# Weight steps tied to their chunk's tanh, score products in turn, and wider attention stages in a fused attention and MLP kernel

## The chip, the core and the metric

The kernel runs on one core of one Trainium2 chip. The metric is the device time of one execution in microseconds, lower is better; the median of several runs counts. The engines are TensorE (PE), VectorE (DVE), ScalarE (ACT), GpSimd (POOL) and SyncE (SP), which issues the transfers.

## What is computed

```python
B, H, S, D = 4, 8, 576, 64
scores = q @ k.T / sqrt(D)             # per head; key within the last 64 positions
attn = exp(scores - max); attn /= sum + 1e-9
x = (attn @ v)                         # as 2304 tokens x 512
xn = x / sqrt(mean(x * x) + 1e-6) * rms_g
h = (silu(xn @ w_gate) * (xn @ w_val)) @ w_out     # d_ff 1536
t = h @ w_in2                                      # d_ff 2048
out = (t * sigmoid(1.702 * t)) @ w_out2
```

All of it is float32. The matrix products of the two MLPs are made as three products of split operands (high and low part).

## The kernel before

The 2304 tokens are six blocks of 384. Each block of the first MLP goes through 12 chunks of 128 hidden columns in two passes of six: in the first pass over the blocks chunks 0 to 5, with the attention of the next block woven in; in the second pass chunks 6 to 11. The second MLP then runs six blocks of 16 chunks. A chunk (L534 on) is a gate product `psg` of 12 matrix products (`proj`, L388), a tanh on ACT (L540), a combine on DVE (L541) that frees the bank of `psg`, a value product `psv` in the same form, a combine (L545), the split of the result in two parts (L548 on ACT, L549 on DVE), and 12 output products (`emit_O`, L509) one chunk later. `psg` and `psv` have one bank each.

Attention works in 18 stages `m` of 128 tokens. The steps of a stage are the transposes of its keys and queries (`att_Tk`, `att_Tq`: L234 and L243 on PE, copies L228 on ACT), 32 score products of 64x64 (`att_S`, L263) into two banks, one per parity of head (`e`), then eight reduces on DVE (L281), eight exps on ACT (L293) and the scaling (L303 to L305), transposes of the result (`att_PT`, L313), value products (`att_PV`, L328), the copy to `xraw` (L336 or L338), the squares (`rms_sq`, L345 to L349), and, once a block, the RMS scaling (`rms_scale`: products with `ones` L359, L362, POOL L363, L365, L369) and the split of the block into `xh` and `xl` (`split_x`, L377 to L381). `at_slot` puts each step into one of 18 slots of a block's first pass, three per chunk; the first three stages stand at the start, before any chunk. Their tiles come from a pool of two PSUM banks. `NLD` = 4 load buffers hold keys, queries and values in the order of `ld_order`.

The weights are float32 in HBM and are split on the chip by 34 weight steps (`w_step`: ACT L142 and L143, DVE L144, L145 and L148; then `w_half`: ACT L126 and DVE L127). 9 of them belong to the first half of the first MLP, 18 to the first MLP as a whole. Slots call them: in block 0 every even slot, up to step 9, later two per block. Three staging buffers hold what SP has loaded.

The order of each engine's instructions is set by a scheduler that simulates the program. `tc.issue_after(ins)` puts what is written in it behind `ins` on the queue of `ins`' engine. Before, the first of the steps 2 to 9 alone, on ACT, is put behind `hold[0]`, which is the last ACT cast of the first block's split; the others stand where the scheduler puts them. `pe_hold` is the last product of the start's RMS scaling.

Of the kernel before, what the change touches and what calls it, by code (L numbers as in the profile page):

```python
# [12 lines left out]
AF = mybir.ActivationFunctionType  # L13
# [4 lines left out]
N_FREE = 1  # L18
# [5 lines left out]
def window_attention__gated_mlp__mlp_kernel(  # L24
# [86 lines left out]
    def w_load(limit):  # L111
        while w_next[0] < min(limit, n_w):
# [6 lines left out]
            staged.append(st)  # L119

    def w_half():
        if not half:
            return
        pair, w24 = half.pop()
        w = wp.tile([128, 2, 1024], F32R, tag="w", name="w")
        nc.scalar.copy(w[:, 0, :], w24.bitcast(F32))  # L126
        nc.vector.tensor_tensor(w[:, 1, :], w24.bitcast(F32), w[:, 0, :].bitcast(F32), ALU.subtract)  # L127
        for e, key in enumerate(pair):
            weights[key] = w[:, :, e * 512:(e + 1) * 512]

    def w_step(limit):
# [8 lines left out]
        m = tmp.tile([128, 1024], I32, tag="tmp", name="m")  # L140
        with tc.issue_after(hold[0]) if N_FREE < w_next[1] <= n_wh else nullcontext():
            nc.scalar.mul(hi.bitcast(F32), hi.bitcast(F32), 2.0 ** -112)  # L142
# [16 lines left out]
    for m in range(lead):  # L159
        ld_order += [("v", 2 * m), ("v", 2 * m + 1)]  # L160
    for m in range(lead, NG // 2):
        ld_order += [("k", m), ("q", m), ("v", 2 * m), ("v", 2 * m + 1)]
    ld_next = [0]
# [93 lines left out]
    def att_S(m):  # L257
        QT = qts[m]
        banks = [att_bank("s") for _ in range(2)]
        for hp in range(NHP):  # L260
            for g in range(2):
                for e in range(2):
                    nc.tensor.matmul(  # L263
                        banks[e][64 * g:64 * g + 64, hp * 128:(hp + 1) * 128],
                        QT[64 * e:64 * e + 64, hp, 64 * g:64 * g + 64],
                        KT[64 * e:64 * e + 64, hp, key_blocks(2 * m + g), :],
                        start=True,
                        stop=True,
                    )
        first = next((g for g in range(2) if (2 * m + g) % GPB == 0), None)  # L270
# [152 lines left out]
    def at_slot(j, s, fn):  # L423
        slots.setdefault(j * NS + s, []).append(fn)
# [8 lines left out]

    def first_S(m):
        with tc.issue_after(pe_hold):
            att_S(m)

    for b in range(1, NB):
        for i in range(TB // 128):
            m = b * TB // 128 + i  # L440
            s0 = 4 * i if b == 1 else 6 * i - 4
            lag = 3
            at_slot(b - 1, s0, lambda m=m: (first_S if m == TB // 128 else att_S)(m))
            if m + 1 < NG // 2:
                at_slot(b - 1, s0 + 2, lambda m=m + 1: att_Tk(m))
                at_slot(b - 1, s0 + 3, lambda m=m + 1: att_Tq(m))
            at_slot(b - 1, s0 + lag, lambda m=m: att_PT(m))
            at_slot(b - 1, s0 + lag + 1, lambda m=m, b=b, i=i: att_PV(m, x_of(b)[0], i * 128))
            at_slot(b - 1, s0 + lag + 2, lambda b=b, i=i: rms_sq(x_of(b)[0], i * 128, x_of(b)[1]))
        at_slot(b - 1, s0 + lag + 3, lambda b=b: rms_scale(*x_of(b), 0, TB))  # L450

    if True:
# [30 lines left out]
        for m in range(T0 // 128):  # L483
            att_S(m)
            att_Tk(m + 1)
            att_Tq(m + 1)
        for m in range(T0 // 128):
# [11 lines left out]
        for ps_i in range(2):  # L499
            f_lo, f_hi = ps_i * FH, (ps_i + 1) * FH  # L500
            for j in range(NB):
# [32 lines left out]
                for f in range(f_lo, f_hi):  # L534
# [4 lines left out]
                    a = ap_.tile([128, TB], F32, tag="a", name="a")  # L539
                    nc.scalar.activation(a, psg[:, :T], AF.Tanh, scale=0.5)  # L540
                    nc.vector.scalar_tensor_tensor(a, a, 1.0, psg[:, :T], ALU.add, ALU.mult)  # L541
# [129 lines left out]
```

## Time and profile before

| | us |
|---|---|
| median of 3 runs | 1056.81 |
| range of the runs | 1056.78 to 1059.46 |
| profiled execution | 1059.42 |
| its span | 1057.6 |
| PE busy in the span | 1010.6 |

The profile is one execution. Busy times of an engine are sums of its instructions; a window of the trace gives them for a stretch. "PEclk" is the granted clock of TensorE as a share of full speed. An idle time in brackets behind a row is what the engine stood before the instruction, with what ended it.

### The profile page before, as it was taken

The numbers are of one execution on the slowest core, as the hardware profiler recorded it, in microseconds if no ns is written. First come the engines' busy times: TensorE is split into PE (matmuls) and PEld (weight loads), VectorE is DVE, ScalarE is ACT, GpSimd is POOL, SyncE is SP. The second block draws the span as 40 slices with busy tenths as digits, with TensorE's granted clock in tenths as the row PEclk, the third lists the DMA queues.
The fourth block names the chain that finished last, engine by engine and source line by source line (L and its number), as shares of the span: only waits on it lengthen the run. The fifth ranks groups of instructions, "written<-read, shape, count | busy, mean of one in ns | idle before, by whom it ended". The sixth has DMA issues, their size and how long they took to land. (4 is left out here: it accounts for less than half of the span.)

```text
span 1057.6 us, 15454 instructions
## 1 busy us (share of the span) xinstructions
PE 1010.6 (96%) x6158; PEld 938.8 (89%) x6158; DVE 515.6 (49%) x1132; ACT 411.0 (39%) x884; POOL 13.2 (1%) x39
## 2 busy tenths in 40 slices
PE   6888599999999989999999999999999999999997
PEld 5778499898989989999999998899999989988896
DVE  5598983645445489644334389232232332322222
ACT  6688874543444346511112145222222222322222
POOL 2000000000000000000000000000000000000000
PEclk9599699898999999999999999999999999999999
DMA  9476971423223065522022052001010010000000
GB/s 236 128 210 209 274 224 41 122 59 100 62 70 90 2 226 175 167 90 86 5 90 90 29 180 100 1 10 50 1 60 1 1 60 1 29 2 2 31 1 30
DMA packets 113320, 88.43 MB, mean 84 GB/s; under 512 B 77664, under 2 KB 104288, under 8 KB 113248
## 3 DMA queue, kind: packets, MB, share of 16 engines
q1 hardware_dynamic: 113248, 87.44, 27.9%
q8 instruction: 48, 0.79, 0.3%
q14 instruction: 24, 0.20, 0.1%
HBM read 68.55 MB, written 18.87 MB: 83 GB/s over the span
## 5 line engine op out<-in xcount | busy, mean ns | idle before, releaser
L614 DVE TENSOR_TENSOR a<-a,psh 128x384 f32<-128x384 f32 x96 | 53.1, 553 | 207.8 <-ACT a L613 207.8
L598 PE MATMUL acc<-w,gh 128*128 128x512 f32 x576 | 153.0, 397 | 0.0
L388 PE MATMUL psh<-x2h,w 128*128 128x384 f32 x768 | 152.6, 339 | 0.2 <-DVE a L614 0.2
L388 PEld LDWEIGHTS psh<-x2h,w 128*128 128x128 f32 x768 | 137.2, 188 | 3.2 <-DVE a L614 0.5
L613 ACT ACTIVATE a<-psh 128x384 f32<-128x384 f32 x96 | 47.1, 491 | 223.7 <-PE psh L388 223.0
L598 PEld LDWEIGHTS acc<-w,gh 128*128 128x128 f32 x576 | 107.1, 188 | 18.5
L509 PE MATMUL acc<-ah,w 128*128 128x384 f32 x576 | 118.9, 343 | 0.3 <-ACT ah L548 0.3
L509 PEld LDWEIGHTS acc<-ah,w 128*128 128x128 f32 x576 | 102.8, 190 | 1.3 <-ACT ah L548 0.8
L541 DVE SCALAR_TENSOR_TENSOR a<-a,psg 128x384 f32<-128x384 f32 x72 | 39.7, 551 | 106.6 <-ACT a L540 106.4
L388 PE MATMUL psh<-x2l,w 128*128 128x384 f32 x384 | 86.2, 338 | 0.0
L598 PE MATMUL acc<-w,gl 128*128 128x512 f32 x288 | 85.2, 396 | 0.0
L540 ACT ACTIVATE a<-psg 128x384 f32<-128x384 f32 x72 | 35.4, 491 | 118.5 <-PE psg L388 118.5
L618 DVE TENSOR_TENSOR gl<-a,gh 128x384 fp32r<-128x384 f32 x96 | 53.5, 558 | 55.6 <-ACT gh L617 45.0
L388 PE MATMUL psg<-xh,w 128*128 128x384 f32 x288 | 69.0, 374 | 11.0 <-ACT xh L379 5.6
L617 ACT CAST gh<-a 128x384 fp32r<-128x384 f32 x96 | 49.3, 513 | 67.9 <-DVE a L614 51.1
L388 PEld LDWEIGHTS psh<-x2l,w 128*128 128x128 f32 x384 | 69.9, 188 | 5.9
L388 PEld LDWEIGHTS psg<-xh,w 128*128 128x128 f32 x288 | 55.1, 206 | 16.1 <-ACT xh L379 7.7
L548 ACT CAST ah<-a 128x384 fp32r<-128x384 f32 x72 | 36.9, 512 | 75.4 <-DVE a L545 75.1
L509 PE MATMUL acc<-al,w 128*128 128x384 f32 x288 | 65.7, 342 | 0.0
L388 PE MATMUL psv<-xh,w 128*128 128x384 f32 x288 | 65.4, 355 | 0.2 <-DVE a L545 0.2
L598 PEld LDWEIGHTS acc<-w,gl 128*128 128x128 f32 x288 | 54.2, 189 | 12.6
L388 PE MATMUL psv<-x2h,w 128*128 128x384 f32 x288 | 58.5, 339 | 0.1
(104 smaller groups left out, 1460.3 us busy)
## 6 DMA issues: line engine op xcount, KB each, us to landing
st<-in_moe_w_out_dram SPq DMA_DIRECT2D x28, 512.0 KB, 5.1
o<-x2s SPq DMA_DIRECT2D x48, 192.0 KB, 1.9
st<-in_moe_w_in_dram SPq DMA_DIRECT2D x16, 512.0 KB, 5.0
st<-in_moe_w_gate_dram SPq DMA_DIRECT2D x12, 512.0 KB, 4.9
st<-in_moe_w_val_dram SPq DMA_DIRECT2D x12, 512.0 KB, 5.8
qkv<-in_v_dram SPq DMA_DIRECT2D x20, 256.0 KB, 3.0
x<-xraw SPq DMA_DIRECT2D x6, 768.0 KB, 4.7
xr<-x SPq DMA_DIRECT2D x6, 768.0 KB, 4.3
```

The source lines that it names most:

```text
L388: nc.tensor.matmul(ps[:, :T], w[:, wi, c * 128:(c + 1) * 128], xx[:, c, :T], start=(i == 0), stop=(i == 3 * KC - 1),)
L509: nc.tensor.matmul(acc[c][:, :T], w[:, wi, c * 128:(c + 1) * 128], aa, start=(f == f_lo and pi == 0), stop=(f == f_hi - 1 and pi == 2),)
L540: nc.scalar.activation(a, psg[:, :T], AF.Tanh, scale=0.5)
L541: nc.vector.scalar_tensor_tensor(a, a, 1.0, psg[:, :T], ALU.add, ALU.mult)
L548: nc.scalar.copy(ah, a)
L598: nc.tensor.matmul(acc[c], (gh, gh, gl)[pi][:, c * 128:(c + 1) * 128], w[:, (0, 1, 0)[pi], :], start=(f == 0 and pi == 0), stop=(f == NF2 ...
L613: nc.scalar.activation(a[:, :T], psh[:, :T], AF.Sigmoid, scale=1.702)
L614: nc.vector.tensor_tensor(a[:, :T], a[:, :T], psh[:, :T], ALU.mult)
L617: nc.scalar.copy(gh[:, :T], a[:, :T])
L618: nc.vector.tensor_tensor(gl[:, :T], a[:, :T], gh[:, :T].bitcast(F32), ALU.subtract)
```

## The change

The change has four parts. First, the ACT part of every weight step after the first is put behind `hold[0]`, and `hold[0]` is the tanh of the chunk in which the step is called, except in block 0, where it stays the last cast of the split. Second, the 32 score products of a stage are chained on PE, so that head pair by head pair and quarter by quarter (the two halves `g` of the queries, the two parities `e` of heads) each stands behind the one before. Third, the slots of an attention stage lie further apart, and a block's stages begin earlier. Fourth, keys and queries of the second block's first stage are transposed in slot 0 of block 0, behind `pe_hold`, instead of at the start; and loads of keys and queries now come before the values of the stage before.

```diff
-        with tc.issue_after(hold[0]) if N_FREE < w_next[1] <= n_wh else nullcontext():
+        with after(hold[0] if w_next[1] > N_FREE else None):
             nc.scalar.mul(hi.bitcast(F32), hi.bitcast(F32), 2.0 ** -112)
...
+    ld_order += [("k", lead), ("q", lead)]
     for m in range(lead, NG // 2):
-        ld_order += [("k", m), ("q", m), ("v", 2 * m), ("v", 2 * m + 1)]
+        if m + 1 < NG // 2:
+            ld_order += [("k", m + 1), ("q", m + 1)]
+        ld_order += [("v", 2 * m), ("v", 2 * m + 1)]
...
+        prev = None
         for hp in range(NHP):
-            for g in range(2):
-                for e in range(2):
-                    nc.tensor.matmul(
+            for g, e in ((0, 0), (0, 1), (1, 0), (1, 1)):
+                with after(prev):
+                    prev = nc.tensor.matmul(
...
-    def first_S(m):
+    def held(fn, m):
         with tc.issue_after(pe_hold):
-            att_S(m)
-
+            fn(m)
+
+    m = TB // 128
+    for fn in (att_Tk, att_Tq):
+        at_slot(0, 0, lambda m=m, fn=fn: held(fn, m))
     for b in range(1, NB):
         for i in range(TB // 128):
             m = b * TB // 128 + i
-            s0 = 4 * i if b == 1 else 6 * i - 4
-            lag = 3
...
+            if b == 1:
+                s0, lags = 1 + 4 * i, (2, 3, 4, 5, 5, 6)
+            else:
+                s0, lags = 6 * i - 7, (2, 3, 5, 7, 8, 9)
+                if b == 2 and i == 0:
+                    s0, lags = -5, (2, 3, 3, 5, 6)
...
+            at_slot(h, s0 + lags[2], lambda m=m: att_PT(m))
+            at_slot(h, s0 + lags[3], lambda m=m, b=b, i=i: att_PV(m, x_of(b)[0], i * 128))
+            at_slot(h, s0 + lags[4], lambda b=b, i=i: rms_sq(x_of(b)[0], i * 128, x_of(b)[1]))
+        at_slot(h, s0 + lags[5], lambda b=b: rms_scale(*x_of(b), 0, TB))
...
         for m in range(T0 // 128):
             att_S(m)
-            att_Tk(m + 1)
-            att_Tq(m + 1)
+            if m + 1 < T0 // 128:
+                att_Tk(m + 1)
+                att_Tq(m + 1)
...
-                    nc.scalar.activation(a, psg[:, :T], AF.Tanh, scale=0.5)
+                    tanh = nc.scalar.activation(a, psg[:, :T], AF.Tanh, scale=0.5).ins
+                    if ps_i or j:
+                        hold[0] = tanh
```

The order of instructions moves in three places that matter below. The first is ACT at the start, around the first weight's scaling; `quad`, `p` and `sm` are the scores, `pt`, `KT` and `QT` the transposed tiles, `st` a weight. Before:

```order
L293 ACTIVATE quad,sm<-quad,sm 128x128 x2
L228 COPY pt<-ps_t 128x512
L293 ACTIVATE quad,sm<-quad,sm 128x128 x2
L228 COPY pt<-ps_t 128x512
L142 ACTIVATE st<-st 128x1024
L143 ACTIVATE st<-st 128x1024
L293 ACTIVATE quad,sm<-quad,sm 128x128 x5
L228 COPY quad<-ps_t 128x512
L293 ACTIVATE quad,sm<-quad,sm 128x128 x3
```

The same place after (L234 for L228, L300 for L293, L145 and L146 for L142 and L143):

```order
L234 COPY pt<-ps_t 128x512
L300 ACTIVATE quad,sm<-quad,sm 128x128 x8
L234 COPY pt<-ps_t 128x512
L300 ACTIVATE quad,sm<-quad,sm 128x128 x4
L145 ACTIVATE st<-st 128x1024
L234 COPY quad<-ps_t 128x512
L300 ACTIVATE quad,sm<-quad,sm 128x128
L146 ACTIVATE st<-st 128x1024
L300 ACTIVATE quad,sm<-quad,sm 128x128 x2
```

The weight's scaling now stands behind five more of the start's exps. The second place is ACT around the tanh of block 0's last chunk. Before, weight steps stand behind it:

```order
L540 ACTIVATE a<-psg 128x384
L228 COPY QT<-ps_q 128x512
L126 CAST w<-m 128x1024 x2
L548 CAST ah<-a 128x384
L228 COPY pt<-ps_t 128x512
L142 ACTIVATE st<-st 128x1024
L143 ACTIVATE st<-st 128x1024
L228 COPY pt<-ps_t 128x512
L142 ACTIVATE st<-st 128x1024
L143 ACTIVATE st<-st 128x1024
L582 ACTIVATE x2s<-acc_548 128x384
L336 COPY xraw<-ps_v 128x4x128
```

After (L559 is the tanh, L569 the cast of L548, L603 the output's copy, L343 the copy of L336):

```order
L559 ACTIVATE a<-psg 128x384
L234 COPY pt<-ps_t 128x512
L569 CAST ah<-a 128x384
L234 COPY pt<-ps_t 128x512
L146 ACTIVATE st<-st 128x1024
L603 ACTIVATE x2s<-acc_532 128x384
L300 ACTIVATE p,sm<-p,sm 128x128 x8
L343 COPY xraw<-ps_v 128x4x128
L603 ACTIVATE x2s<-acc_534 128x384
L352 ACTIVATE s_1197<-xraw 128x512
L234 COPY KT<-ps_k 128x4x128
L234 COPY QT<-ps_q 128x512
```

No weight is cast any more in this place, and a stage's eight exps stand in a row. The third place is PE at a score stage; the number behind `ps_s` is its bank's tile. Before, at the boundary from block 2 to 3:

```order
L509 MATMUL acc2_1330<-al_1868,w_1216 128x384
L509 MATMUL acc3_1331<-al_1868,w_1216 128x384
L263 MATMUL ps_s_1798<-KT_93,QT_92 64x128 x8
L359 MATMUL ps_r_1783<-ones_88,sq_1349 128x1
L263 MATMUL ps_s_1799<-KT_93,QT_92 64x128 x8
L365 MATMUL ps_r_1783<-ident_87,ry_1788 128x128 x3
L234 MATMUL ps_k_1883<-ident_87,qkv_1745 128x128 x4
L388 MATMUL psg_1962<-xh_1871,w_558 128x384
```

After, at a stage of block 0:

```order
L320 MATMUL ps_t_741<-ident_87,p_635 128x128 x4
L320 MATMUL ps_t_748<-ident_87,p_635 128x128 x4
L270 MATMUL ps_s_755<-KT_93,QT_92 64x128
L395 MATMUL psg_794<-xh_520,w_717 128x384 x4
L270 MATMUL ps_s_756<-KT_93,QT_92 64x128
L270 MATMUL ps_s_755<-KT_93,QT_92 64x128
L270 MATMUL ps_s_756<-KT_93,QT_92 64x128
L270 MATMUL ps_s_755<-KT_93,QT_92 64x128
```

The products into one bank stood together, and now the two banks alternate from the second product on. (One row of this listing can stand for two instructions of the trace.)

## Rows read from the trace of the kernel before

**Rows 1.** Page, busy time and share of the span per engine.

```profile
PE 1010.6 (96%) x6158; PEld 938.8 (89%) x6158; DVE 515.6 (49%) x1132; ACT 411.0 (39%) x884; POOL 13.2 (1%) x39
```

**Rows 2.** Windows: length, busy PE, PEld, DVE, ACT, POOL, PEclk, DMA share, GB/s.

```profile
0.00:46.60 46.60, 34.08 (x330) 28.47 (x330) 20.98 (x92) 28.53 (x78) 7.89 (x34) 0.75 0.84 190
46.60:105.26 58.66, 52.13 (x376) 48.56 (x372) 54.78 (x118) 48.53 (x100) 0.00 (x0) 0.94 0.69 202
105.26:141.80 36.54, 23.93 (x184) 20.81 (x184) 36.35 (x65) 29.76 (x50) 1.90 (x1) 0.72 0.77 246
415.00:1057.60 642.60, 636.17 (x3315) 594.59 (x3313) 250.36 (x439) 178.32 (x328) 0.00 (x0) 1.00 0.14 49
```

**Rows 3.** Timeline of the start (start, duration, idle before): ACT, SP, PE.

```profile
21.21 1.10 ACT L142 ACTIVATE st<-st 128x1024 f32<-128x1024 f32 x1 [3.13 <-DMA st<-in_moe_w_val_dram]
...
34.18 0.58 ACT L228 COPY quad<-ps_t 128x512 f32<-128x512 f32 x1 [0.23 <-PE ps_t L313]
37.13 1.16 ACT L143 ACTIVATE st<-st 128x1024 int32<-128x1024 uint32 x1 [2.37 <-DMA st<-in_moe_w_val_dram]
...
40.46 0.63 ACT L345 ACTIVATE s<-xraw 128x512 f32<-128x512 f32 x1
...
29.31 1.28 SPq L201 DMA_DIRECT2D qkv<-in_k_dram  x2
...
22.30 0.66 PE L234 MATMUL ps_k<-ident,qkv 128*128 128x128 f32 x4 [2.66 <-DMA qkv<-in_k_dram]
...
46.61 0.69 PE L388 MATMUL psg<-xh,w 128*128 128x384 f32 x1
```

**Rows 4.** Windows of the exps alone (L293, ACT), then the reduces (L281, DVE).

```profile
46.60:105.26 58.66, 9.92 (x48) 0.94 0.69 202
...
46.60:105.26 58.66, 5.55 (x48) 0.94 0.69 202
```

**Rows 5.** Weight steps on DVE: windows of L144 and L145, timeline DVE, PE.

```profile
46.60:105.26 58.66, 6.71 (x10) 0.94 0.69 202
105.26:141.23 35.97, 4.03 (x6) 0.72 0.78 249
...
46.60:105.26 58.66, 12.09 (x10) 0.94 0.69 202
...
104.01 1.22 DVE L148 CUSTOM_DVE_ANT_0 m<-st,m 128x2048 uint16<-128x2048 uint16 x1
...
108.44 2.35 DVE L127 TENSOR_TENSOR w<-m,w 128x1024 fp32r<-128x1024 f32 x2
...
141.82 1.68 PE L388 MATMUL psg<-xh,w 128*128 128x384 f32 x8 [0.21 <-DVE a L541]
```

**Rows 6.** Timeline of the boundary from block 4 to 5, DVE and PE.

```profile
364.72 0.69 DVE L338 COPY xraw<-ps_v 128x512 f32<-128x512 f32 x1 [2.16 <-PE ps_v L328]
...
366.64 0.29 DVE L349 TENSOR_TENSOR sq<-s 128x128 f32<-128x128 f32 x1
...
369.05 0.28 PE L359 MATMUL ps_r<-ones,sq 128*128 128x1 f32 x2
...
373.11 0.45 PE L388 MATMUL psg<-xh,w 128*128 128x384 f32 x1 [1.60 <-ACT xh L379]
```

**Rows 7.** Boundary from block 2 to 3: two windows, and the timeline of PE.

```profile
248.20:262.66 14.46, 12.83 (x81) 11.33 (x80) 9.20 (x33) 6.79 (x25) 0.85 (x1) 0.76 0.48 147
251.00:257.00 6.00, 5.58 (x33) 4.77 (x34) 4.30 (x17) 4.51 (x18) 0.00 (x0) 0.56 0.35 103
...
251.03 1.34 PE L263 MATMUL ps_s<-KT,QT 64*64 64x128 f32 x16 [1.12 <-DVE sm L281]
...
255.19 0.69 PE L388 MATMUL psg<-xh,w 128*128 128x384 f32 x1 [0.40 <-ACT xh L379]
```

**Rows 8.** Timeline of PE: score products of a start stage and of a later one.

```profile
15.68 1.10 PE L263 MATMUL ps_s<-KT,quad 64*64 64x128 f32 x32
...
68.21 1.09 PE L263 MATMUL ps_s<-KT,QT 64*64 64x128 f32 x16
```

More of the change, by code (lines that the diff above doesn't have):

```diff
@@ L119, in w_load, with after @@
             staged.append(st)
+    def after(ins):
+        return tc.issue_after(ins) if ins is not None else nullcontext()
     def w_half():
@@ L268, in att_S @@
                         stop=True,
-                    )
+                    ).ins
         first = next((g for g in range(2) if (2 * m + g) % GPB == 0), None)
@@ L440, in window_attention__gated_mlp__mlp_kernel @@
             m = b * TB // 128 + i
-            s0 = 4 * i if b == 1 else 6 * i - 4
-            lag = 3
-            at_slot(b - 1, s0, lambda m=m: (first_S if m == TB // 128 else att_S)(m))
-            if m + 1 < NG // 2:
[L445 to L450, printed above, removed]
+            if b == 1:
[4 more added lines that the diff above has]
+                    s0, lags = -5, (2, 3, 3, 5, 6)
+            h = b - 1
+            if m == TB // 128:
+                at_slot(h, s0, lambda m=m: held(att_S, m))
+            else:
+                at_slot(h, s0, lambda m=m: att_S(m))
+            if m + 1 < NG // 2:
+                at_slot(h, s0 + lags[0], lambda m=m + 1: att_Tk(m))
+                at_slot(h, s0 + lags[1], lambda m=m + 1: att_Tq(m))
+            at_slot(h, s0 + lags[2], lambda m=m: att_PT(m))
+            at_slot(h, s0 + lags[3], lambda m=m, b=b, i=i: att_PV(m, x_of(b)[0], i * 128))
+            at_slot(h, s0 + lags[4], lambda b=b, i=i: rms_sq(x_of(b)[0], i * 128, x_of(b)[1]))
+        at_slot(h, s0 + lags[5], lambda b=b: rms_scale(*x_of(b), 0, TB))
     if True:
```

## The prediction

> **What bounds the kernel now.** I read the busy shares first: TensorE (PE) is busy 96% of the span [rows 1], so only the stretches in which it is not at work, or not at full clock, can give anything. The windows by stage [rows 2] say where those are. From 415 us to the end PE works 636.17 of 642.60 us at a granted clock of 1.00, and the order of all engines is the same there in both kernels: nothing to win or lose. Three stretches ahead are different. In the start (0 to 46.6 us) PE has 34.08 us at a clock of 0.75 and ScalarE (ACT) and the transfers set the pace. In block 0 up to the combine (L541) of its sixth chunk (46.6 to 105.26) VectorE (DVE) is busy 54.78 of 58.66 us. From there to block 1's second chunk (105.26 to 141.8) DVE is busy 36.35 of 36.54 us, and PE does 23.93 at 0.72. Those 141.8 us are where the waits are; between 142 and 415 PE is near its limit except at the block boundaries.
>
> The sum is made against the profiled execution, 1059.42 us (span 1057.6 and 1.82 around it). The median of the runs is 1056.81, 2.61 lower, and I take the same savings off it. Under 0.3%, about 3.2 us, a measurement of this kernel can't tell a change from none.
>
> **A, the start: -3.4.** ACT reaches the first weight's scaling (L142) at 21.21 after standing 3.13 us for its DMA, with exps of stage 2 queued behind it [rows 3]. The changed order has 21 of the 24 start exps ahead of the corresponding instruction, 16 before, and the two copies of the second block's first keys and queries are gone from the start. An exp costs 0.41 us (9.92 over 24, [rows 4]), so 5 x 0.41 = 2.1 and two copies of about 0.57 each = 1.1: the last transposed copy, at 34.18, comes 3.2 us earlier. The PE wait of 2.66 us at 22.30 for the block's keys goes with them. What is late next is the fourth ACT weight instruction (L143, at 37.13 after 2.37 us for its DMA): in the new order it stands between the copy of xraw and the Square of 40.46. SP issues that DMA some 1.3 us earlier, since the two half loads of k(4) (1.28 us at 29.31) no longer stand right ahead of it, so about 35.8 + 1.16 = 37.0, against 40.46: -3.4. The moved transposes (4 in 0.66, twice) come ahead of the first gate product in place of stage 3's score products. First gate product: 46.61 becomes about 43.2. If the DMA lands when it did, I get -2.2; if it doesn't bind, -6. The DMA queue (SP) is passed too: k(4) and q(4) now come before v(6) and v(7), and the latter wait for the release of k(3) and q(3); the value products that need them are some 20 us later, so I cost that at nothing; were that cover gone it would be one load, about 2.66.
>
> **B, block 0 to the sixth combine: -3.7.** Weight steps cost DVE, per step, 6.71/10 = 0.67 (L144), 12.09/10 = 1.21 (L145), 1.22 (L148) and 2.35/2 = 1.18 (L127) [rows 5]: 4.28 us. Now every step waits for the tanh of its chunk or, in block 0, for the last cast of the first block's split; by the sixth combine the order has 2 L144, 2 L145 and 1 L148 fewer (-1.3 - 2.4 - 1.2 = -5.0) and one scaling of a stage's exps (L304, L305) more, which I put at +1.3 since L305 passes over 1024 columns as L145 does. DVE's 54.78 becomes 51.1; with the same 3.9 idle the stretch takes 55.0 instead of 58.7. From 52 (no idle) to 58.7 (ACT or the weight's DMA takes over) is possible. Behind the tied L142 on ACT stand L143, exps and copies, and for it waits the weight chain of DVE, not PE until that weight's chunk comes; that is why I cost the tie itself at nothing.
>
> **C, from there to block 1's second chunk: -12.5.** Six whole weight steps (6 L144 in 4.03, [rows 5]) stand here before and none now: 6 x 4.28 = 25.7 of DVE's 36.35 us. DVE then has about 10.7 us of work and no longer bounds; the chain into the next block does. 16 output products at 0.21 (8 of a like shape in 1.68, [rows 5]) and the score products 1.1 beside transposes: +5. Then the eight exps of the stage, now in a row on ACT, 8 x 0.41 = 3.3: +8.3. The last copy of xraw, the Square and the two sums took from 364.72 to 366.93 at a boundary without neighbours [rows 6], 2.2, with half a us of latency: +11. From the first product with ones to the first gate product there took 369.05 to 373.11, 4.06 [rows 6]: +15.1. From a block's first gate product to its second chunk's took 255.19 to 262.66, 7.5 [rows 7], and the one stage of score products and reduces that falls into it (reduces 5.55/3 = 1.85 per stage, [rows 4]) costs perhaps 1.5: 24 us instead of 36.5. Bounds: 19 (PE's 23.93 at a clock of 0.72 is 17.2 at 1.00, plus 1.60 of idle) and 28.5 (each of the eight exps and reduces is paid in full on the way). Second chunk: 141.82 becomes 122.2.
>
> **D, the boundaries from block 1 to 4: -1.0.** Each loses about 4.7 us [rows 7]: 14.46 - 12.83 = 1.63 idle, and 12.83 x (1 - 0.76) = 3.1 by the clock, 0.56 in six of these us, a mean between the two levels of 2.4 and 1.2 GHz. The 1.12 us wait for the second bank of scores goes, as the boundary's score stage now has its banks in turn; but on ACT eight exps (3.3) instead of four (1.65) stand ahead of the next tanh, which takes away 1.65. So each lies between +0.5 and, if PE stays warm and only the 1.60 of [rows 6] is left, -3.1; for three of them between +1.5 and -9.3. I take a third of 1.12 each, -1.0, since the rms chain that sets the first gate product is untouched. The boundary 4 to 5 has no score stage: 0.
>
> **E, score products in turn: -11.1.** Stage 2 in the start ran 32 score products in 1.10 us; 15 later stages show two groups of 16, one bank each, of 1.09 [rows 8]. The changed order alternates the banks in all of them: the first product, then 15 when the second bank is free, then 16. So 2 x 1.09 - 1.10 = 1.08 less, minus the single product that stands alone, 1.09/16 = 0.07: 1.01. Stages 7 to 17 lie in the PE-bound stretch, 11 x 1.01 = 11.1; stages 3 to 6 are in A to C. The price of it is that the 15 products, and the output products queued behind them on PE, wait until DVE has freed the second bank; before, 16 products waited there as well (1.12 us at 251.03, [rows 7]), so I add nothing. Bounds 0 to 11.9.
>
> A rule speaks against E. The Trainium skill, TensorEngine Tiling (Array Packing), "PSUM Bottleneck", says that tiling speeds up TensorE but not the evacuation of PSUM, which can become the limit after it; by that rule E would be 0. Its "Tiling Modes" has four independent 64x64 tiles, with which the 1.10 against 2.18 us of [rows 8] agree.
>
> **Sum.** 3.4 + 3.7 + 12.5 + 1.0 + 11.1 = 31.7: 1056.81 - 31.7 = 1025.1 (for an execution like the profiled one 1027.7). The second MLP stays at 642.6 us.
>
> **Rivals.** *More at start and boundaries* (0.20): PE stays at full clock through three boundaries (9.3 instead of 1.0) and the weight's DMA doesn't bind in the start (6.0 instead of 3.4): 10.9 more, 1014.2. For it speaks that a stall is what precedes the drop of 0.56; against it that ones to first gate product still leaves PE 1.60 us idle where no score stage stands. *Block 0 stays as long* (0.15): DVE gets lighter but waits for ACT and for the weights' DMA instead, B is 0 and C only 8: 1033.3. For it: ACT is busy 48.53 of 58.66 in B [rows 2]; against it: DVE is the busier. *Packing is hidden* (0.05): DVE's reduces take 1.85 us a stage, more than the 1.01 saved, so if PE waits for them anyway, E is 0: 1036.2. Against it: DVE is busy 49% of the span [rows 1], most of it early, and PE has other products to go on with. *Slower* (0.05): the tanh of a chunk stands behind eight exps, and PE has a single bank for the gate product, so each stage could stall PE up to 3.3 us. It decides from 31.7/15 = 2.1 us per stage on; at the full 3.3, 15 x 3.3 = 49.5 is lost and 31.7 won: 1074.6. Against it: the bank is needed again only after a value product and an output product, 12 + 12 products at up to 0.21, some 5 us. That the order isn't what the diff says is excluded by the order shown above.
>
> **Chances and range.** The forecast has 0.55, the rivals 0.20, 0.15, 0.05 and 0.05. The forecast's own bounds, A 2.2 to 6, B 0 to 6.7, C 8 to 17.5, D -1.5 to 9.3, E 10 to 11.9, don't fall together; half of their width around the sum and the first three rivals give 1009 to 1040. Faster by over 0.3%: 0.94, from all but the slower rival and 0.01 of the others; within it 0.02 (several terms at their poor ends); slower 0.04.
>
> **What would show it.** First gate product near 43 (A); about 55 us to the sixth combine (B); no L147 (the shift of before's L144) between block 0's sixth combine and block 1's second chunk, which starts near 122 (C); each stage's score products after the first block in one stretch of 1.1 us, but for the first product (E); boundaries of 13 to 14 us (D); 642.6 us for the second MLP. The prediction is wrong if PE's waits before a gate product grow to some us in each stage (tanh behind exps), if the sixth combine stays near 105, or if PE stays busy just as long in the later blocks though the products are packed.

## The result, and the profile of the changed kernel

The changed kernel takes 1032.69 us (median of 4 runs, 1028.16 to 1033.24), the kernel before 1057.84 beside it; the ratio is 0.9752, interval 0.972 to 0.9783. The profiled executions are 1032.62 and 1059.42 us: 26.8 us less, with spans of 1030.8 and 1057.6. 1025.1 was predicted, with a range of 1009 to 1040, and 31.7 us less. All times of stretches below are of one profiled execution each.

In the changed kernel the lines have moved: L559 is the tanh, L562 the combine that frees the bank of `psg`, L270 the score products, L288 the reduces, L300 the exps, L310 to L312 their scaling, L345 the copy to `xraw`, L366, L370, L372 and L376 the RMS chain, L386 the cast to `xh`, L145 and L146 the weight step on ACT, L395 the projections, L528 the output products.

The page's first part after, against [rows 1]: PE works 22 us less, DVE 1 and ACT 3 us less.

```profile
PE 988.7 (96%) x6158; PEld 916.8 (89%) x6158; DVE 514.5 (50%) x1132; ACT 408.1 (40%) x884; POOL 12.4 (1%) x39
```

The windows after that answer to [rows 2], cut at the same events (first gate product, sixth combine, second gate product of block 1), and the second MLP; columns as there:

```profile
0.00:44.03 44.03, 32.45 (x298) 27.49 (x299) 20.46 (x91) 27.09 (x75) 7.91 (x34) 0.72 0.86 189
44.03:98.37 54.34, 50.24 (x395) 46.31 (x394) 51.73 (x115) 45.80 (x99) 0.00 (x0) 0.91 0.68 200
98.37:125.04 26.67, 21.57 (x218) 17.89 (x216) 15.16 (x58) 14.87 (x48) 0.86 (x1) 0.94 0.59 164
388.40:1030.80 642.40, 635.91 (x3312) 593.98 (x3310) 268.47 (x456) 194.85 (x344) 0.00 (x0) 1.00 0.16 56
```

The third row is the plainest: DVE was busy 36.35 of 36.54 us there, and now 15.16 of 26.67. The events themselves, from the timelines of ACT, PE and DVE:

```profile
37.37 1.13 ACT L146 ACTIVATE st<-st 128x1024 int32<-128x1024 uint32 x1 [1.59 <-DMA st<-in_moe_w_val_dram]
...
44.03 0.67 PE L395 MATMUL psg<-xh,w 128*128 128x384 f32 x1
...
98.37 0.55 DVE L562 SCALAR_TENSOR_TENSOR a<-a,psg 128x384 f32<-128x384 f32 x1
...
125.04 1.68 PE L395 MATMUL psg<-xh,w 128*128 128x384 f32 x8 [1.12 <-DVE a L562]
```

| stretch | before | after | change | predicted |
|---|---|---|---|---|
| A, to the first gate product | 46.61 | 44.03 | -2.6 | -3.4 |
| B, to the sixth combine | 58.65 | 54.34 | -4.3 | -3.7 |
| C, to block 1's second gate product | 36.56 | 26.67 | -9.9 | -12.5 |
| the rest of the span (D and E) | 915.8 | 905.8 | -10.0 | -12.1 |

By stretches the sum looks like a good forecast with each term a little off. The experiments show that this holds for one of its five terms. How far one execution can be trusted shows in two pairs of kernels of the experiments. The changed kernel and a_chain_inner have the same order of instructions up to 117 us, and A took 44.0 and 42.6 us in them, B 54.3 and 52.8. The kernels a_nochain and best2 have the same order up to 330 us, and C took 26.3 and 29.0. Differences of that size in one stretch say little.

### The profile page after: what moved, and what is told of

Read it like the earlier page. It is cut to its first block, busy times and chain, and to the rows that moved or that the text cites. A ratio compares the mean times of both kernels' runs of the same rounds, so it can differ in the third digit from the quotient of the medians.

```text
span 1030.8 us, 15447 instructions
## 1 busy us (share of the span) xinstructions
PE 988.7 (96%) x6158; PEld 916.8 (89%) x6158; DVE 514.5 (50%) x1132; ACT 408.1 (40%) x884; POOL 12.4 (1%) x39
## 5 line engine op out<-in xcount | busy, mean ns | idle before, releaser
L395 PE MATMUL psh<-x2h,w 128*128 128x384 f32 x768 | 152.6, 339 | 0.2 <-DVE a L635 0.2
L395 PEld LDWEIGHTS psh<-x2h,w 128*128 128x128 f32 x768 | 137.2, 188 | 3.2 <-DVE a L635 0.5
L528 PE MATMUL acc<-ah,w 128*128 128x384 f32 x576 | 116.2, 341 | 0.3 <-ACT ah L569 0.3
L528 PEld LDWEIGHTS acc<-ah,w 128*128 128x128 f32 x576 | 101.7, 188 | 1.0 <-ACT ah L569 0.6
L562 DVE SCALAR_TENSOR_TENSOR a<-a,psg 128x384 f32<-128x384 f32 x72 | 39.6, 551 | 105.0 <-ACT a L559 105.0
L395 PE MATMUL psh<-x2l,w 128*128 128x384 f32 x384 | 86.2, 338 | 0.0
L395 PE MATMUL psg<-xh,w 128*128 128x384 f32 x288 | 65.9, 360 | 13.1 <-DVE a L562 7.7
L395 PEld LDWEIGHTS psh<-x2l,w 128*128 128x128 f32 x384 | 69.9, 188 | 5.9
L395 PEld LDWEIGHTS psg<-xh,w 128*128 128x128 f32 x288 | 51.5, 195 | 19.9 <-DVE a L562 8.9
L559 ACT ACTIVATE a<-psg 128x384 f32<-128x384 f32 x72 | 35.2, 489 | 84.5 <-PE psg L395 84.5
L619 PEld LDWEIGHTS acc<-w,gl 128*128 128x128 f32 x288 | 54.3, 189 | 12.6
L528 PE MATMUL acc<-al,w 128*128 128x384 f32 x288 | 64.1, 342 | 0.0
L569 ACT CAST ah<-a 128x384 fp32r<-128x384 f32 x72 | 36.9, 512 | 68.7 <-DVE a L566 68.6
L395 PE MATMUL psv<-xh,w 128*128 128x384 f32 x288 | 62.6, 348 | 0.2 <-DVE a L566 0.2
L395 PE MATMUL psv<-x2h,w 128*128 128x384 f32 x288 | 59.1, 340 | 0.1
```

The lines of the kernel that those rows point to most:

```text
L395: nc.tensor.matmul(ps[:, :T], w[:, wi, c * 128:(c + 1) * 128], xx[:, c, :T], start=(i == 0), stop=(i == 3 * KC - 1),)
L528: nc.tensor.matmul(acc[c][:, :T], w[:, wi, c * 128:(c + 1) * 128], aa, start=(f == f_lo and pi == 0), stop=(f == f_hi - 1 and pi == 2),)
L559: tanh = nc.scalar.activation(a, psg[:, :T], AF.Tanh, scale=0.5).ins
L569: nc.scalar.copy(ah, a)
L619: nc.tensor.matmul(acc[c], (gh, gh, gl)[pi][:, c * 128:(c + 1) * 128], w[:, (0, 1, 0)[pi], :], start=(f == 0 and pi == 0), stop=(f == NF2 ...
```

## Experiments

Ratios are to the kernel before, with 95% intervals; 0.001 is 1.06 us. "Parts" are those of the change: ties of the weight steps, chain of the score products, wider slots, keys with the order of loads. The line numbers of the other kernels are those of the changed one, some lower by a few.

| kernel | ratio | interval |
|---|---|---|
| changed kernel | 0.9752 | 0.972 to 0.9783 |
| without the chain (a_nochain) | 0.9619 | 0.9597 to 0.9641 |
| with the old tie (a_notie) | 0.9768 | 0.9745 to 0.9791 |
| with the old slots (a_noslots) | 1.0121 | 1.0102 to 1.0141 |
| keys at the start, old loads (a_nokeys) | 0.9900 | 0.9878 to 0.9921 |
| keys at the start, new loads (a_keysstart) | 0.9675 | 0.9655 to 0.9695 |
| no chain at the boundary stages (a_chain_inner) | 0.9714 | 0.9691 to 0.9737 |
| no chain, keys at the start (best1) | 0.9681 | 0.9658 to 0.9703 |
| no chain, old tie (nochain_notie) | 0.9720 | 0.9696 to 0.9745 |
| before, with the chain alone (only_chain) | 1.0088 | 1.0064 to 1.0113 |
| before, with the tie alone (only_tie) | 0.9867 | 0.9839 to 0.9896 |
| no chain, later split of a block (best2) | 0.9644 | 0.9615 to 0.9673 |
| as best2, later scaling (best3) | 0.9661 | 0.9628 to 0.9695 |

### The chain

```diff
 # a_nochain
-                with after(prev):
+                with after(None):
                     prev = nc.tensor.matmul(
```

> The changed kernel (1032.7 us, 26.8 us below the kernel before in their profiled executions) with the chain of the score products alone taken out, so that each stage's 32 products stand again in two groups of 16, one bank each. Theory: in the trace of the changed kernel a stage takes two products in 0.43 us and 30 in 1.10 us, of TensorE some 1.4 us, against 2.05 before. With 15 stages the chain is worth 15 x 0.65 = 10 us where TensorE bounds, so 1042 (1040 to 1046), and TensorE's busy time rises by 10 us. Rival (the evacuation of the two banks bounds, reduces of 1.85 us a stage): within 2 us of the changed kernel, 1031 to 1035.

Measured: 0.9619 against 0.9752. Without the chain the kernel is 14 us faster (0.0133 x 1058), not 10 us slower; both theories written down missed. TensorE's busy time is 987.8 us without and 988.7 with the chain: the packing didn't go away. The score products alone (windows of `ps_s`: length, then busy PE, PEld and DVE, clock and transfers) took 39.4 us of PE before, 27.3 with the chain and 29.8 without:

```profile
0.00:1057.60 1057.60, 39.40 (x576) 30.32 (x576) 33.11 (x144) 0.96 0.28 84
...
0.00:1030.80 1030.80, 27.31 (x576) 19.05 (x576) 31.89 (x144) 0.98 0.29 86
...
0.00:1017.30 1017.30, 29.83 (x576) 23.86 (x576) 32.34 (x144) 0.98 0.30 87
```

The timeline of PE shows why, first two rows with the chain, the third without it (start, duration, count; one score product is two rows of the trace):

```profile
211.78 0.43 PE L270 MATMUL ps_s<-KT,QT 64*64 64x128 f32 x2
...
215.69 1.10 PE L270 MATMUL ps_s<-KT,QT 64*64 64x128 f32 x30
...
204.64 1.58 PE L270 MATMUL ps_s<-KT,QT 64*64 64x128 f32 x32
```

Without a chain, in 12 of the 18 stages, the 32 products run in one stretch, here of 1.58 us (by the order of instructions mostly bank after bank, alternating at the end), where the kernel before had 1.09 twice [rows 8]. With the chain they cost 0.43 and 1.10, about the same, but the first product takes its bank at 211.78 and the other 30 rows come 3.9 us later, and no reduce begins before they have run. It isn't the second bank that they wait for: ACT's last copy out of the banks ahead of them had ended at 211.95 (first row below), and PE isn't idle, but runs 19 products of chunks in between. The chain fixes only the sequence of the score products; how far apart they stand is the scheduler's order. In the changed kernel DVE's first reduce of that stage waits for them (second row):

```profile
211.36 0.59 ACT L234 COPY pt<-ps_t 128x512 f32<-128x512 f32 x1 [0.59 <-PE ps_t L320]
...
216.83 0.29 DVE L288 CUSTOM_DVE_ANT_0 p<-ps_s,masks 128x128 f32<-128x128 f32 x1 [1.82 <-PE ps_s L270]
```

What that does to the block's end can be read from the boundary of block 2 to 3. The value products of the stage before, the last of block 3, stand behind these reduces. First the changed kernel's timeline (the last tanh, those value products, the last copy of `xraw`, the scaling of the block, its first gate product), then the same five of the kernel without the chain:

```profile
219.88 0.47 ACT L559 ACTIVATE a<-psg 128x384 f32<-128x384 f32 x1
...
221.33 1.15 PE L335 MATMUL ps_v<-pt,qkv 128*64 128x64 f32 x32
...
224.03 0.69 DVE L345 COPY xraw<-ps_v 128x512 f32<-128x512 f32 x1
...
230.46 2.18 DVE L376 SCALAR_TENSOR_TENSOR xraw<-xraw,g_sb,ps_r 128x384 f32<-128x384 f32 x4
...
232.28 0.44 PE L395 MATMUL psg<-xh,w 128*128 128x384 f32 x1
```

```profile
215.43 0.49 ACT L559 ACTIVATE a<-psg 128x384 f32<-128x384 f32 x1 [1.39 <-PE psg L395]
...
210.76 1.15 PE L335 MATMUL ps_v<-pt,qkv 128*64 128x64 f32 x32
...
212.62 0.68 DVE L345 COPY xraw<-ps_v 128x512 f32<-128x512 f32 x1
...
221.76 2.19 DVE L376 SCALAR_TENSOR_TENSOR xraw<-xraw,g_sb,ps_r 128x384 f32<-128x384 f32 x4 [0.70 <-PE ps_r L372]
...
224.03 0.42 PE L395 MATMUL psg<-xh,w 128*128 128x384 f32 x1
```

With the chain the last copy comes 4.1 us after the last tanh, without it 2.8 us before; the scaling of the block follows the tanh by 10.6 and 6.3 us, and the first gate product by 12.4 and 8.6. Block 2 to 3 (second tanh to second tanh) shows PE idle 3.4 us with the chain (first row, changed kernel) and 0.6 without (second row):

```profile
185.80:244.30 58.50, 55.09 (x470) 50.21 (x468) 36.56 (x106) 31.03 (x86) 0.85 (x1) 1.00 0.46 119
```

```profile
181.40:236.90 55.50, 54.94 (x474) 51.72 (x474) 36.66 (x105) 32.10 (x87) 0.85 (x1) 1.00 0.51 127
```

Whether that is the boundary stage's own doing or a lag that all stages build up was the next question.

```diff
 # a_chain_inner
-                with after(prev):
+                with after(None if m > 6 and m % 3 == 1 else prev):
                     prev = nc.tensor.matmul(
```

> The changed kernel with the chain of the score products taken out of the second stage of each block from the third block on alone (stages 7, 10, 13 and 16, the ones at the boundaries of blocks); the other stages keep it. The changed kernel is at 0.975 of the kernel before, the one without any chain at 0.962. In the traces the boundary from block 2 to 3 (last tanh of the one to second tanh of the next) takes 24.4 us with the chain and 21.5 without, and the last copy of xraw comes 4.1 us after the last tanh with it and 2.8 us before it without. Theory: the chain makes every stage's attention late (the first product takes a bank, the others wait for the second, and the reduces of either bank wait for nearly all 32), so the last stage's squares and the RMS chain of the block are late; taking it out of the boundary's stage alone gives less than a third: 0.971 to 0.975. Rival (it is the boundary's own score stage, which stands between the first gate products and whose exps stand ahead of the tanh): two thirds or more come back, 0.966 or less.

Measured: 0.9714, in the range of the theory of the lag, and not the 0.966 of the rival. By the ratios that is 4 of the 14 us, but the interval overlaps that of the changed kernel, and the profiled execution has its gain of 3.2 us ahead of block 1's second gate product (121.54 against 125.04), while the two kernels' order of instructions is the same up to 117 us. Behind it the two take 906.1 and 905.8 us, and the kernel without any chain 895.4:

```profile
121.54 1.68 PE L395 MATMUL psg<-xh,w 128*128 128x384 f32 x8 [1.11 <-DVE a L562]
```

So the chain of the boundary stages costs nothing that these runs show. In the changed kernel its first product stands only 1.0 us ahead of the rest there (stages 10, 13 and 16; not at all in stage 7), as at the boundary of block 2 to 3:

```profile
231.87 0.43 PE L270 MATMUL ps_s<-KT,QT 64*64 64x128 f32 x2 [0.67 <-ACT pt L234]
...
232.83 1.10 PE L270 MATMUL ps_s<-KT,QT 64*64 64x128 f32 x30
```

In the other stages from 8 on it stands 2.1 to 4.4 us ahead. That those lags make up the cost fits all of this; a kernel that takes the chain out of those stages alone wasn't run.

The same chain in the narrow slots of the kernel before:

```diff
 # only_chain: on the kernel before
         for hp in range(NHP):
-            for g in range(2):
-                for e in range(2):
-                    nc.tensor.matmul(
+            for g, e in ((0, 0), (0, 1), (1, 0), (1, 1)):
+                with after(prev):
+                    prev = nc.tensor.matmul(
```

> The kernel before with the chain of the score products alone. By the sum of the prediction: 11.1 us less, 0.9895. By the theory that the chain makes attention late: with the narrow slots of the kernel before the second bank comes free late, so each of 15 stages holds up its block's RMS chain; slower than before, 1.005 to 1.02, the boundaries from block 1 to 4 some 3 us longer each.

Measured: 1.0088, slower, within the second theory and 20 us from the prediction's sum. Its list of PE's waits has the combine and the squares of the RMS chain at the top (waited for, us in total, times, longest):

```profile
PE psg L392 <- DVE a L549: 13.2, 6, 4.9
PE ps_r L363 <- DVE sq L353: 8.4, 5, 3.7
```

So the chain costs in both kernels, 9 us before and 14 after. The Trainium skill, TensorEngine Tiling (Array Packing), "PSUM Bottleneck", which the prediction set against term E, says that the evacuation of PSUM may become the limit once TensorE is sped up; here DVE stands idle 1.82 us before the reduce above, so what this trace shows is not the reduces' speed but their late start.

### The wider slots

```diff
 # a_noslots
-            if b == 1:
-                s0, lags = 1 + 4 * i, (2, 3, 4, 5, 5, 6)
-            else:
-                s0, lags = 6 * i - 7, (2, 3, 5, 7, 8, 9)
-                if b == 2 and i == 0:
-                    s0, lags = -5, (2, 3, 3, 5, 6)
+            s0, lags = 4 * i if b == 1 else 6 * i - 4, (2, 3, 3, 4, 5, 6)
```

> The changed kernel with the slots of the attention stages as before (lags of 2 to 6 slots, starts at 4 slots' distance in block 1 and 6 later). My sum had no term for the wider stages. Theory from the two traces: they are what keeps TensorE at full clock at the boundaries (granted clock 1.00 in blocks 1 to 3 instead of 0.94 to 0.97), since the chain into the next block no longer starts behind a score stage that has to wait for its second bank; without them three boundaries lose 2 to 3 us each again: 1040 (1037 to 1043), with stretches of clock 0.5 to 0.8 at the boundaries. Rival (the boundaries got warm because of the packed score products): 1031 to 1035 and the clock of blocks 1 to 3 stays at 1.00.

Measured: 1.0121, 39 us slower than the changed kernel and slower than the kernel before; the direction was right and the size five times too small. Each of blocks 1 to 4 takes 66 to 68 us (second tanh to second tanh), where the changed kernel has 58 in blocks 1 to 3 and 53 in block 4. A window of block 2 shows a granted clock of 0.87 where the changed kernel has 1.00, and the list of waits shows what stands at the boundary: PE waits 11 us for the squares.

```profile
197.20:265.40 68.20, 60.19 (x471) 55.20 (x469) 37.35 (x105) 31.02 (x86) 0.85 (x1) 0.87 0.38 101
```

```profile
PE ps_r L366 <- DVE sq L356: 11.0, 5, 4.0
PE ps_t L320 <- DVE p L312: 9.7, 7, 1.9
```

The prediction gave the wider slots no term at all. With the chain in place they are the largest of the four parts. What they give without the chain wasn't tried alone; together with the keys and loads they bring 26 us there, from the tie alone (only_tie, 0.9867) to the kernel without the chain (0.9619).

### Keys and loads

```diff
 # a_nokeys; a_keysstart is the same without the first hunk
-    ld_order += [("k", lead), ("q", lead)]
     for m in range(lead, NG // 2):
-        if m + 1 < NG // 2:
-            ld_order += [("k", m + 1), ("q", m + 1)]
-        ld_order += [("v", 2 * m), ("v", 2 * m + 1)]
+        ld_order += [("k", m), ("q", m), ("v", 2 * m), ("v", 2 * m + 1)]
...
-    for fn in (att_Tk, att_Tq):
-        at_slot(0, 0, lambda m=m, fn=fn: held(fn, m))
...
-            if m + 1 < T0 // 128:
-                att_Tk(m + 1)
-                att_Tq(m + 1)
+            att_Tk(m + 1)
+            att_Tq(m + 1)
```

> The changed kernel with the keys and queries of the second block's first stage transposed at the start again and with the order of loads as before. Theory: the first gate product goes from 44.0 back to 46.6 us, and nothing else changes: 1035.3 (1034 to 1037). Rival (the scheduler's shift in the later loads matters more): more than 5 us; or the earlier gate product is absorbed by VectorE, which bounds block 0: within 1 us of 1032.7.

Measured: 0.990, 16 us slower, where 2.6 was expected, as the first rival has it. Its first tanh is at 46.5 us, earlier than the 49.7 of the changed kernel, not later. The loss is in the blocks, where the old order puts a stage's keys behind the values of the stage before, whose loads have to wait until value products free a buffer (SP stands 67.8 us for that in 12 places); the list of PE's waits:

```profile
PE ps_k L237 <- DMA qkv<-in_k_dram: 17.5, 7, 4.7
```

> The changed kernel with the keys and queries of the second block's first stage transposed at the start again, but with the changed order of loads (which the kernel with all of part four undone did not have: there TensorE waited 17.5 us in 7 places for keys' DMAs). Theory: the loads' order is what counted there, and the move of the two transposes out of the start brings nothing or costs a little (with them at the start the first tanh was at 46.5 and the sixth at 91.9 us, in the changed kernel at 49.7 and 97.9): 0.970 (0.966 to 0.974). Rival (the move itself gives the 17 us): 0.985 or more. Rival two (what block 0 gains is given back at the next boundaries): 0.974 to 0.977, with the sixth tanh at 92 to 94 all the same.

Measured: 0.9675, 8 us faster than the changed kernel. The order of loads is what counts (0.990 to 0.9675, 24 us), as expected; the move of the two transposes itself costs 8 us here. But the reason written down is wrong: its first tanh is at 49.6 and its sixth at 98.4 us, like the changed kernel's, and the gain lies behind block 1's second gate product (899.3 us instead of 905.8), most of all at the last boundary (17.7 instead of 20.2 us from block 4's last tanh to block 5's second). Nor does it add to the gain of the chain's removal:

```diff
 # best1: the edits of a_nochain and a_keysstart
-                with after(prev):
+                with after(None):
...
-    for fn in (att_Tk, att_Tq):
-        at_slot(0, 0, lambda m=m, fn=fn: held(fn, m))
...
```

> The changed kernel without the chain (1019.8 us, 0.962) and with the keys and queries of the second block's first stage transposed at the start; the changed order of loads, the wider stages and the ties of the weight steps stay. If the two gains add: 5 us less than without the chain, 0.957 (0.953 to 0.960). Rival (block 0's earlier end is absorbed at the next boundary): 0.961 to 0.963.

Measured: 0.9681, slower than without the chain alone (0.9619) by 7 us, against both expectations. Its first tanh comes at 53.4 us, 4.5 later, and its first gate product at 46.45 instead of 43.02. The move has opposite signs in the two settings, so what is measured is the order that the scheduler makes around it; which of its steps decides stays open.

### The ties of the weight steps

The edit ties only ACT's first instruction of a step (L145). L146 isn't tied: it starts at 37.37, ahead of the casts of the first block.

```diff
 # a_notie; nochain_notie: the same and the edit of a_nochain
-        with after(hold[0] if w_next[1] > N_FREE else None):
+        with after(hold[0] if N_FREE < w_next[1] <= n_wh else None):
...
-                    if ps_i or j:
-                        hold[0] = tanh
```

> The changed kernel with the tie of the weight steps alone as before (steps 2 to 9 behind the last cast of the split, later ones untied); in the order of instructions 6 weight steps stand again behind the tanh of block 0's last chunk. Theory: the stretch from block 0's sixth tanh (97.9 us in the changed kernel) to the second of block 1 (127.5) goes from 29.6 back towards the 39.8 us of the kernel before, and what VectorE was relieved of before the sixth tanh comes back too: 10 + 3, so 1045 (1041 to 1049). Rival (wider stages alone would have brought the stretch down, the tie is a cover): less than 4 us, 1033 to 1036.

Measured: 0.9768, within the intervals of the changed kernel, so by the number the rival. But the trace shows the theory's stretch: from block 0's sixth tanh to block 1's second it takes 41.8 us, with DVE busy 39.78 (first row), where the changed kernel takes 29.6. The next block is then 2 us shorter, since its weight steps have been done (second row; 58.3 us in the changed kernel):

```profile
96.30:138.10 41.80, 26.40 (x231) 21.93 (x230) 39.78 (x85) 33.76 (x69) 4.04 (x1) 0.80 0.81 240
138.10:194.40 56.30, 54.47 (x471) 50.24 (x470) 37.48 (x107) 33.74 (x89) 0.86 (x1) 1.00 0.53 151
```

So the tie gives 12.2 us in the one stretch and gives 9.0 back in the four blocks behind (2.0, 2.1, 1.9 and 3.0). From that I took it that the tie only spreads the work, and put it to two tests.

> The changed kernel without the chain (0.962 of the kernel before) and with the tie of the weight steps as before; wider stages, moved keys and order of loads stay. With the chain in place, undoing the tie lengthened the way from block 0's sixth tanh to block 1's second from 29.6 to 41.8 us and shortened each of the next three blocks by some 2 us and the boundary 4 to 5 by 2.8. Theory: the tie spreads the same work over the blocks, where TensorE pays for it again; without the chain too its worth is within 4 us: 0.958 to 0.966. Rival (the prediction's 12.5 us are real and the chain hid them): 0.972 to 0.976.

Measured: 0.9720 against 0.9619 without the chain: the tie is worth 10.7 us here, at the edge of the rival's range and outside mine.

```diff
 # only_tie: on the kernel before
-        with tc.issue_after(hold[0]) if N_FREE < w_next[1] <= n_wh else nullcontext():
+        with after(hold[0] if w_next[1] > N_FREE else None):
...
+                    if ps_i or j:
+                        hold[0] = tanh
```

> The kernel before with the tie of the weight steps alone. By the prediction's sum (block 0 and the way to block 1's second chunk) 10 to 16 us less: 0.985 to 0.990. By the theory that the tie only spreads the work: the way from block 0's sixth tanh to block 1's second falls from 39.8 to about 30 us, the three blocks behind grow by 2 us each and the boundary 4 to 5 by 3: about 1 us in all, 0.996 to 1.002.

Measured: 0.9867, 14 us, where the prediction's sum has 16.2 for B and C. The theory that the tie only spreads the work falls. The stretch between the two tanhs, first with the tie alone and then without chain and tie:

```profile
101.60:133.80 32.20, 29.39 (x238) 25.55 (x237) 17.15 (x62) 17.08 (x53) 0.86 (x1) 0.84 0.41 108
```

```profile
93.80:141.60 47.80, 34.30 (x254) 29.07 (x253) 47.07 (x94) 38.97 (x75) 1.23 (x1) 0.75 0.88 265
```

The tie takes 7.6 us out of it in the kernel before (39.8 to 32.2), 18.4 without the chain (47.8 to 29.4) and 12.2 with it; the four blocks behind give back 0.4, 6.6 and 9.0. The term is real, and the price in the later blocks is real too. What decides how much is paid there stays open: a late RMS chain can't be all of it, since the kernel without the chain pays 6.6 too.

### A version that beats both

The kernel without the chain, at 1019.8 us, beats both. Two attempts to go on from it:

```diff
 # best2: with the edit of a_nochain
-                        nxh, nxl = raw_split(0 if end else j + 1, xr)
+                        with after(tanh), after(comb):
+                            nxh, nxl = raw_split(0 if end else j + 1, xr)
...
 # best3 adds: the scaling (L310 to L312) of stages 7, 10, 13, 16 one slot later
+                at_slot(h, s0 + 1, lambda m=m: late_scaling(m))
```

> The changed kernel without the chain, and with the split of a loaded block (raw_split) put behind the tanh and the combine of the chunk in which the program calls it. In the traces of the changed kernel and of the one without the chain the casts and differences of the next block's split stand ahead of the first combine of block 5, and TensorE waits 3.2 to 3.3 us there for that combine, the longest wait for a combine. Theory: that wait goes, 3 us: 0.959 (0.957 to 0.961). Rival (ScalarE's weight cast and the loads keep it): 0.961 to 0.963.

Measured: 0.9644, no gain. The wait stayed, 3.35 us: ACT's copy of an output (L604) waits 7.43 us for the store of an earlier one, and the tanh stands behind it. The split had been in front of the combine, but was not what held it.

```profile
339.90 0.49 ACT L604 ACTIVATE x2s<-acc 128x384 f32<-128x384 f32 x1 [7.43 <-DMA o<-x2s]
...
341.41 0.81 PE L395 MATMUL psg<-xh,w 128*128 128x384 f32 x2 [3.35 <-DVE a L562]
```

> As best2, and the scaling of the exps of the boundary stages (7, 10, 13, 16) one slot later, behind the combine of the first chunk of the next block. In the changed kernel the scaling (1.22 us and two short ones) stands ahead of that combine at two boundaries, where TensorE waits 1.1 and 1.9 us for it. If those waits are all that the scaling costs: 1 to 3 us less than best2, 0.957. Rival (the later scaling makes the stage's transposes and value products late, and the block's RMS chain with them): at or above best2.

Measured: 0.9661, within the intervals of best2: nothing gained, as the rival has it. Blocks 2 and 3 take 57.0 and 56.7 us, 55.4 and 55.1 in best2.

## Why the prediction was right, and where it was not

**The sum**, 31.7 us, came out 5 us larger than what the profiled executions show and 6.5 larger than the medians' difference, inside the range. Of its five terms the experiments show the stated cause for one, C. The part of the change behind E costs time instead of saving it, D's gain went into waits, and what shortened A and B is only in part what the prediction names.

**A, start.** -2.6 of -3.4, near the bound for a DMA that lands when it did: the weight's L146 starts at 37.37 (37.13 before), not at 35.8. The step that failed in this execution is the SP queue's 1.3 us: the loads of keys and queries went ahead of the load of `g_sb` instead of away, and the weight's DMA was issued at 32.50, 31.98 before (second row).

```profile
32.50 0.51 SPq L118 DMA_DIRECT2D st<-in_moe_w_val_dram  x1
...
31.98 0.51 SPq L118 DMA_DIRECT2D st<-in_moe_w_val_dram  x1
```

In a_chain_inner, with the same order there, it was issued at 29.72, L146 started at 35.99 and the first gate product at 42.63, so the miss is no larger than what two executions differ by. The two reasons don't add up as the sum has them. The five more exps ahead of the first weight come with the chain (21 in every kernel with it, 16 in every one without). With the chain the move of the keys isn't needed: with keys at the start again the first gate product comes at 42.84 (a_keysstart) and 39.73 (a_nokeys). Without the chain the move alone gives 3.4 us (46.45 in best1, 43.02 in a_nochain).

**B, block 0.** -4.3 of -3.7: DVE's busy time fell as counted, 54.78 to 51.73, and its idle time from 3.9 to 2.6 us. But that the tie brought it isn't shown for the changed kernel: with the old tie (a_notie) three more of DVE's weight instructions stand in the stretch, DVE is busy 53.92 us, and it takes 54.22 all the same. The tie alone on the kernel before takes 2.8 us off it (58.65 to 55.87), and without the chain 2.6.

```profile
43.98:98.20 54.22, 50.98 (x411) 47.33 (x410) 53.92 (x117) 47.65 (x102) 0.00 (x0) 0.94 0.75 219
```

**C, into block 1.** -9.9 of -12.5. The mechanism is the one named: DVE falls from 36.35 to 15.16 us of work, and with the old tie (a_notie) the stretch is back at 37.34, with DVE at 35.32. The chain behind it was sized too short: exps were counted once, but the first combine of block 1 waits behind the next stage's exps and scaling too, 1.12 us at 125.04. What the sum left out is the price of the six steps in the later blocks; it costs "the tie itself at nothing". That price is 9.0 us against a kernel with the old tie.

**D, boundaries.** The clock did what the rival hoped: it is 1.00 in blocks 1 to 3, where [rows 7] had 0.56 in six of 14.46 us. The stretch of [rows 7], from the last output product to the second gate product, is nonetheless 14.47 us after:

```profile
227.22:241.69 14.47, 11.06 (x114) 8.62 (x111) 9.86 (x36) 9.13 (x27) 0.85 (x1) 1.00 0.69 215
```

More products lie in it (114, 81 before), and what the clock gave went into waits: PE idle 3.4 us, 1.63 before. The clock is kept by the wider slots, for which the sum had no term (0.87 in block 2 with the old ones); the waits are the chain's, since without it PE is idle 0.6 us in all of block 2 to 3.

**E, packing.** The step that failed, and the one that mattered. Per stage the products take 0.43 and 1.10 us instead of 1.09 twice, so 0.65 less and not 1.01, since the product that stands alone took 0.43 and not 0.07. Most of this gain comes without the chain too: of the 12.1 us that the score products lost in all (39.4 to 27.3), 9.6 stay without it. The chain's own worth is 14 us the other way. I priced the wait for the second bank at nothing because "before, 16 products waited there as well", and looked only at who waits on PE; the ones who wait are the reduces, the exps and at the end the RMS chain, and in the stage shown not for the bank but for products that the scheduler put 3.9 us behind the first one.

**The rivals.** The slower rival, a tanh behind eight exps, is there in small: PE's wait for that combine rose from 4.1 to 7.7 us, 5 waits.

```profile
PE psg L395 <- DVE a L562: 7.7, 5, 3.3
```

*Packing is hidden* was nearer to the truth on E than its 0.05, though by another way: it has PE waiting for the reduces, and the runs show the reduces waiting for PE.

**What the parts are worth.** Taken out of the changed kernel one by one: slots 39 us, keys and loads 16, tie 2, chain -14. They sum to some 43, not 26, and the tie is worth 14 alone, 11 without the chain and 2 with it. There is no single worth of a part here; a sum over terms that fits can be an accident, and this one was in part: the loss by the chain, at nothing in the sum, stands against the slots, which weren't in it and gave more than that.

## What to carry to other kernels

A chain of instructions fixes their sequence, not that they stand next to each other: look in the order how far the first stands ahead of the rest, who waits for their result, and how far that consumer is from a chain that ends a block. In this kernel wider slots gave most of the packing without a chain. And before crediting a term to a part of a change, undo that part alone: a good total hides terms with the wrong sign.

## What the runs showed of the hardware

The 32 score products of a stage (64x64) took 1.10 us in full alternation of the two banks and 1.09 for the 16 of one bank alone [rows 8]. In one stretch, mostly bank after bank, the 32 took 1.58 us (204.64), and a single product 0.43 (211.78). So 1.09 twice overstates what the second bank's products cost right behind the first's; whether the banks overlap or each group has a fixed part, no run here separates. TensorE's granted clock was 1.00 over blocks 1 to 3 of the changed kernel, with PE idle 3.4 of 58.5 us in block 2, and 0.87, a mean between its two levels of 1.2 and 2.4 GHz, in block 2 of the kernel with the old slots, where PE is idle 8.0 of 68.2.
